# Column 0 multiplied centred and scaled afterwards, with the identity made on GpSimd and the first rows loaded in two halves

## The chip, the cores and the metric

The kernel runs on one core of a Trainium2 chip. The metric is the device time of one execution in microseconds (us). The profiled span, from the first to the last instruction of the profile, is about 1.7 us shorter than that time. Ratios, medians and ranges: runs that count as slow (over 1.5% above the fastest of their kernel) are left out. Absolute times are compared within one chip only: the kernel before takes 179.2 to 180.3 us, depending on the chip.

A ratio is the mean time of one kernel's fast runs over the mean of the kernel before's fast runs of the same rounds, so it is not quite the ratio of the medians quoted beside it.

A load is *issued* when its queue takes it up and *lands* when its last byte has arrived; rows are *usable* when the first instruction that waits for them, the statistics on DVE, starts. The PE clock is *open* at full pace and *closed* at half pace.

Engines: PE is TensorE (PEld its weight loads), DVE is VectorE, ACT is ScalarE, POOL is GpSimd, SP is SyncE, which only issues loads and stores here.

## The reference, cut to what matters

```python
x  = A_x                                   # 1 x 2048 x 512, bf16
xn = (x - mean) / sqrt(var + 1e-5)         # over the 512
B  = (gelu(xn @ w_gate) * (xn @ w_up)) @ w_down      # 512 -> 1792 -> 512
A  = irfft2(rfft2(xn) * (w_r + 1j * w_i))            # a filter over both axes
out = x + A + B
```

The kernel cuts the 2048 rows into 16 "columns" of 128 rows. The first two products, `g` (gate) and `u` (up), need `xn` of a column transposed, and weight chunks of 128 output features. The filter's row tables come partly from six GpSimd gathers.

## The kernel before

A small list scheduler inside the kernel orders the instructions of each engine by priorities and estimated durations. The start is what the change touches. Loads (cut):

```python
    load_x(0, 1)                                    # 128 rows x 512, 128 KB, SyncE
    d_ident = load_ct("ident", "ident", "ACT")      # identity for transposes, 32 KB
    load_x(1, 1)
    load_w(0, 2, ("SP", "ACT"))                     # Wg and Wu, chunks 0 and 1: 256 KB each
    ...
    load_x(2, 2)
    load_w(2, 4)
    ...
```

Layer norm of a column, then transposes on PE (cut):

```python
s  = bn_stats(x_t[:, c]);  ag = bn_aggr(s)          # DVE: mean and variance
e  = tensor_scalar(var + EPS)                       # DVE
r  = nc.gpsimd.tensor_tensor(ve, half, op=pow)      # POOL: 1/std
xn = tensor_scalar(x_t, mean, rstd, subtract, mult) # DVE, in two halves
...  # nc.tensor.transpose x4, copied to xnT by ACT and DVE; then glu(c)
```

While PE has nothing useful to do it multiplies a constant tile ("warm"), which is meant to have its clock open in time (here this starts at 1.34 us, and the clock opens at 7.11). The gathers wait for column 11 to be normalised:

```python
            d_tw.append(dma(P * n * 2, lambda ...: gather(k, s, c, a, n),
                            [g_idx] + XN[11], 20, eng="POOL", issue=1.2))
```

Of the kernel before, what the change touches and what calls it, by code (L numbers as in the profile page):

```python
# [10 lines left out]
P = 128  # L11
# [6 lines left out]
S = 2048  # L18
# [106 lines left out]
class _Op:  # L125
    __slots__ = ("eng", "dur", "fn", "deps", "prio", "new", "use", "lag", "n", "start", "end", "kind", "nbytes")


class _Plan:
# [7 lines left out]
    def op(self, eng, dur, fn, deps=(), prio=0.0, new=(), use=(), lag=0.0, nbytes=0):  # L137
        o = _Op()
        o.eng, o.dur, o.fn, o.prio, o.lag, o.nbytes = eng, dur, fn, prio, lag, nbytes
        o.deps = [d for d in deps if d is not None]  # L140
        o.new = list(new)
        o.use = list(new) + [b for b in use if b not in new]
        for b in o.use:
            b.users += 1
        o.n, o.start, o.end = len(self.ops), None, None
        self.ops.append(o)
        return o

    def run(self):
# [11 lines left out]
        while left:  # L161
            nxt, moved = None, False
            for e, ops in waiting.items():
                if not ops:
                    continue
                if t_eng[e] > now + 1e-9:
                    nxt = t_eng[e] if nxt is None else min(nxt, t_eng[e])
                    continue
                best = None
                for o in ops:  # L170
                    if any(d.end is None for d in o.deps):
                        continue
                    at = max([d.end + d.lag + self.HOP for d in o.deps if d.eng != "PE" or o.eng != "PE"] + [0.0])
                    if o.nbytes and o.eng != "POOL" and len(lanes) >= 8:
                        at = max(at, sorted(lanes)[-8])
                    if at > now + 1e-9:
                        nxt = at if nxt is None else min(nxt, at)
                        continue
                    held = [rings[b.tag][-self.bufs[b.tag]] for b in o.new if len(rings[b.tag]) >= self.bufs[b.tag]]
                    if any(b.free is None for b in held):  # L180
                        continue
                    at = max([b.free for b in held] + [0.0])
                    if at > now + 1e-9:
                        nxt = at if nxt is None else min(nxt, at)
                        continue
                    if best is None or (o.prio, o.n) < (best.prio, best.n):
                        best = o
                if best is None:
                    continue
                o, moved = best, True  # L190
                o.start = now
                o.end = now + o.dur
                t_eng[e] = o.end
                if o.nbytes:
                    wire = max(wire, o.end + 1.0) + o.nbytes / 0.34e6
                    o.end = wire + 1.0
                    if o.eng != "POOL":
                        lanes.append(o.end)
                    lanes = [x for x in lanes if x > now]
                for b in o.new:  # L200
                    rings[b.tag].append(b)
                for b in o.use:
                    b.left -= 1
                    if not b.left:
                        b.free = o.end + o.lag + self.HOP
                ops.remove(o)
                order.append(o)
                left -= 1
# [10 lines left out]
def kernel(  # L219
# [36 lines left out]
    Bs = pc.tile([P, 4, 2 * NG, NC, 2, 4], BF16, name="Bs", tag="Bs")  # L256
    RF_t = pc.tile([P, NC, P], BF16, name="RF_t", tag="RF")
# [7 lines left out]
    eps = pc.tile([P, 2], F32, name="eps")  # L265
    tiles = {}

# [45 lines left out]
    def load_x(c0, n, eng="SP", deps=()):  # L313
        q = nc.sync if eng == "SP" else nc.scalar
        o = load(n * P * D * 2, lambda: q.dma_start(out=x_t[:, c0:c0 + n], in_=x_v[:, c0:c0 + n]), deps, eng=eng)
        for c in range(c0, c0 + n):
            XD[c] = o

    def load_w(f0, f1, engs=("SP", "SP")):
        a, b = f0 * P, f1 * P  # L320
        os = []
        for t, v, e in ((Wg_sb, wg_v, engs[0]), (Wu_sb, wu_v, engs[1])):
            q = nc.sync if e == "SP" else nc.scalar
            os.append(load(NE * P * P * 2 * (f1 - f0),
                           lambda t=t, v=v, q=q: q.dma_start(out=t[:, :, a:b], in_=v[:, :, a:b]), eng=e))
        for f in range(f0, f1):
            WD[f] = os
# [6 lines left out]
    load_x(0, 1)  # L334
    d_ident = load_ct("ident", "ident", "ACT")
    load_x(1, 1)
    load_w(0, 2, ("SP", "ACT"))
    add("ACT", 1.3, lambda: nc.scalar.activation(out=eps[:, 1:2], in_=eps[:, 0:1], func=AF.Gelu_apprx_tanh),
        (o_eps,), -900)
    load_x(2, 2)  # L340
    load_w(2, 4)
    load_w(4, 6)
    load_x(4, 4)
    load_w(6, 10)
    load_x(8, 4)
    load_w(10, 14)
# [15 lines left out]
    def gather(k, s, c, a, n):  # L362
# [5 lines left out]
    Wd_sb = pc.tile([P, NFC, D], BF16, name="Wd_sb")  # L368
# [3 lines left out]
    o_mem = [add("POOL", 0.3, lambda: nc.gpsimd.memset(warm[:], 1.0), (), -20, lag=0.05),  # L372
             add("POOL", 0.2, lambda: nc.gpsimd.memset(half[:], -0.5), (), -15, lag=0.05)]  # L373
    wb = _Buf("S")
    NWARM, NGAP, GAP = 10, 1, 4
# [15 lines left out]
    XN, XT = {}, {}  # L391
# [6 lines left out]
    def layernorm(c0, n, due, after=(), halves=1):  # L398
        k = slice(c0, c0 + n)
        ag = []  # L400
        for c in range(c0, c0 + n):
            s = dve(0.6, lambda c=c: stats(c), [XD[c]] + list(after), due - 3.0 + 0.01 * (c - c0))
            ag.append(dve(0.15, lambda c=c: V.bn_aggr(out=mv[:, c], in_=tiles["st", c][:]), (s,), due - 3.2, ))
        e = dve(0.07, lambda: V.tensor_scalar(  # L404
            out=ve[:, k], in0=mv[:, k, 1], scalar1=EPS, scalar2=None, op0=ALU.add), ag, due - 5)
        r = add("POOL", 0.55, lambda: nc.gpsimd.tensor_tensor(  # L406
            out=rstd[:, k], in0=ve[:, k], in1=half[:, k], op=ALU.pow), (e, o_mem[1]), due - 5, lag=0.1)
        for c in range(c0, c0 + n):
            XN[c] = []
            for h in range(halves):  # L410
                d = slice(h * D // halves, (h + 1) * D // halves)
                XN[c].append(dve(0.04 + 0.29 / halves, lambda c=c, d=d: V.tensor_scalar(  # L412
                    out=xn[:, c, d], in0=x_t[:, c, d], scalar1=mv[:, c, 0:1], scalar2=rstd[:, c:c + 1],
                    op0=ALU.subtract, op1=ALU.mult), (r,), due - 2.5))
        return ag

    def pe_transpose(c, due):
        XT[c] = []
        b = _Buf("S")
        n = len(XN[c])  # L420
        for h in range(n):
            es = range(h * NE // n, (h + 1) * NE // n)

            def mm(h=h, es=es):
                if h == 0:
                    psum(f"tp.{c}", [P, NE, P], BF16)
                for e in es:
                    nc.tensor.transpose(tiles[f"tp.{c}"][:, e], xn[:, c, e * P:(e + 1) * P], ident)

            def ev(es=es, eng=(nc.scalar.copy, V.tensor_copy)[h]):  # L430
                eng(out=xnT[c // 4][:, es[0]:es[-1] + 1, c % 4], in_=tiles[f"tp.{c}"][:, es[0]:es[-1] + 1])

            o = pe(0.24 / n, mm, (XN[c][h], d_ident), due - 2, new=(b,) if h == 0 else (), use=(b,))
# [6 lines left out]
    first = layernorm(0, 1, -28, (), 2)  # L440
    layernorm(1, 1, -25, first)
    for c in range(4):
        if c == 2:
            layernorm(2, 2, -22, XT[0])
        pe_transpose(c, -28 + 3 * c)
        if c < NGAP:
            dummies(GAP, -29.9 + 3 * c, XN[c], P)
    for c0, n, due in ((4, 2, 14), (6, 2, 16), (8, 4, 24), (12, 4, 32)):
        layernorm(c0, n, due)
        for c in range(c0, c0 + n):  # L450
            dma_transpose(c, due)
        if c0 == 6:
            d_rf = load(P * NC * P * 2, lambda: nc.sync.dma_start(
                out=RF_t[:], in_=rf_d.rearrange("p (c k) -> p c k", c=NC)), XN[7])
            load_x(12, 4, deps=XN[7])
# [5 lines left out]
    for k in range(2):  # L461
        for c, s, a, n in ((2, 1, 0, 7 * KC), (0, 0, 0, KC), (1, 1, 7 * KC, KC)):
            d_tw.append(dma(P * n * 2, lambda k=k, c=c, s=s, a=a, n=n: gather(k, s, c, a, n),
                            [g_idx] + XN[11], 20, eng="POOL", issue=1.2))
# [20 lines left out]

    def glu(c0, n, f0, nf=1, extra=()):
# [10 lines left out]
        def mm(nm, W, tag, a, b):  # L497
            if a == 0:
                psum(f"{nm}.{key}", [P, D], tag=tag)
            for f in range(a, b):  # L500
                for e in range(NE):
                    nc.tensor.matmul(tiles[f"{nm}.{key}"][:, f * w:f * w + w], lhsT=W[:, e, (f0 + f) * P:(f0 + f + 1) * P],  # L502
                                     rhs=rhs(e), start=(f + e == 0), stop=(f == nf - 1 and e == NE - 1),
                                     skip_group_check=nf > 1)

        g = [o for c in range(c0, c0 + n) for o in XT[c]]
        step = min(nf, 2)
        us = []
        for a in range(0, nf, step):
            deps = g[-1:] if a else g  # L510
            new = [([], []), ([gb], [ub])][a == 0]
            g = [pe(step * dur, lambda a=a: mm("g_ps", Wg_sb, "G", a, a + step), deps + [WD[f0 + a][0]], t,
                    new=new[0], use=(gb,))]
            us = [pe(step * dur, lambda a=a: mm("u_ps", Wu_sb, "U", a, a + step), us + g + [WD[f0 + a][1]], t,
# [22 lines left out]
    FIRST = [(0, 1, 0, 4), (1, 1, 0, 4), (0, 2, 4, 2), (2, 2, 0, 2), (2, 2, 2, 2), (2, 2, 4, 2)]  # L537
    for c, n, f, nf in FIRST + [(0, 4, f, 1) for f in range(6, NFC)]:
# [8 lines left out]
    def fold(cg, t):  # L547
# [27 lines left out]
        for q in range(4):  # L575
            sb = _Buf("S")

            def mm(q=q):
                bp, xf = psum(f"bp.{cg}.{q}", [P, 4, P]), tiles[f"xf.{cg}"]
                for j in range(4):  # L580
                    nc.tensor.matmul(bp[:, j], lhsT=xf[:, j, q, :], rhs=RF_t[:, 4 * cg + j, :], start=True, stop=True)  # L581

            def ev(q=q):
                o = Bs[:, q].rearrange("p g c r a -> p (c r) g a")[:, 8 * cg:8 * cg + 8]
# [32 lines left out]
    def dstep(G, t):  # L617
        sb, db = _Buf("S"), _Buf("ds")

        def mm():  # L620
            dp = psum(f"dp.{G}", [P, 2, 2, P])
            work(f"ds.{G}", [P, D], "ds")
            for q in range(4):
                nc.tensor.matmul(dp[:, q % 2, q // 2], lhsT=Bs[:, q, G].rearrange("p c r a -> p (c r a)"),  # L624
# [173 lines left out]
    def load_ri():  # L798
# [4 lines left out]
    d_wd = [dma(P * 7 * D * 2, lambda k=k: nc.sync.dma_start(  # L803
        out=Wd_sb[:, 7 * k:7 * k + 7], in_=wd_v[:, 7 * k:7 * k + 7]), [PS_[3, q] for q in range(4)], 71 + k)
        for k in range(2)]
# [48 lines left out]
    def down(c, t):  # L854
# [8 lines left out]
        for k in range(len(cuts) - 1):  # L863
# [5 lines left out]
            def mm(k=k, s=s, tag=tag):  # L869
                y = psum(f"yp_.{c}.{k}", [P, D], tag=tag)  # L870
                for f in range(NFC):
                    nc.tensor.matmul(y[:, s], lhsT=tiles[sb, f][:, cl * P:(cl + 1) * P], rhs=Wd_sb[:, f, s],  # L872
# [54 lines left out]
```

## Time and profile before

| | before |
|---|---|
| time, median of 3 runs | 180.27 us (180.09 to 180.38) |
| profiled span (of a further run, which took 179.39 us) | 177.6 us |
| PE busy | 173.4 us, 98% |
| first byte of a load | 1.72 us |
| first useful matmul | 6.89 us |

The page's first part, busy time and share of the span:

```profile
span 177.6 us, 3041 instructions
PE 173.4 (98%) x1100; PEld 92.9 (52%) x1100; DVE 118.1 (66%) x266; ACT 87.4 (49%) x158; POOL 18.6 (10%) x33
```

The chain of waits of the kernel before, its first 12 us; columns are start, duration and what ran:

```profile
1.34 4.44 PE warm L380 x10
5.79 0.64 PE tp L428 x4
...
6.89 0.82 PE g_ps L502 x8
7.72 0.45 PE u_ps L502 x8
8.16 0.22 PE tp L428 x4
8.39 0.45 PE g_ps L502 x8
8.83 0.01 issue
8.84 0.62 PE u_ps L502 x8
9.46 0.45 PE g_ps L502 x8
...
10.80 0.45 PE u_ps L502 x8
11.25 0.45 PE tp L428 x8
```

From 1.34 us on the whole chain is PE. The first eight g matmuls take 0.82 us and every later eight 0.45: the clock opens in between, at 7.11 us. From there on nothing is lost but 0.18 us at 8.84, for Wu chunks 2 and 3, and 0.28 us near 76. So only the time ahead of the useful work can be won. By 11.25 us both columns 0 and 1 have their first g and u.

The timeline of DVE before, where the rows arrive (start, duration, instruction, and in brackets how long the engine stood idle and for what):

```profile
3.51 0.69 DVE L396 BATCH_NORM_STATS2 st<-x_t 128x6 f32<-128x512 bf16 x1 [3.51 <-DMA x_t<-in_A_x_dram]
5.38 0.60 DVE L412 TENSOR_SCALAR xn<-x_t,mv,rstd 128x256 bf16<-128x256 bf16 x2
```

### The profile page before, as it was taken

What the parts mean: (1) busy time and instruction counts of PE and PEld (TensorE: products, weight loads), DVE (VectorE), ACT (ScalarE), POOL (GpSimd) and SP (SyncE); (2) the same over time, 40 slices, a digit from 0 to 9 for tenths busy, and PEclk for the clock granted to TensorE, in tenths of its full rate; (3) what the DMA queues carried; (4) which work ended last, traced back from release to release, by engine and by line L of the source; (5) the groups of instructions that cost most, each with busy time, mean ns of one, the idle gap of its engine ahead of it and who ended that gap; (6) DMA issues with size and microseconds to landing.
All of it is one profiled execution on the core that took longest, in us unless ns stands there. A gap on an engine that the chain in (4) does not pass through costs nothing.

```text
span 177.6 us, 3041 instructions
## 1 busy us (share of the span) xinstructions
PE 173.4 (98%) x1100; PEld 92.9 (52%) x1100; DVE 118.1 (66%) x266; ACT 87.4 (49%) x158; POOL 18.6 (10%) x33
## 2 busy tenths in 40 slices
PE   6999999999999999999999999999999999999993
PEld 2598545545554544554555455554445444544463
DVE  1869999999537995889999885336442541632522
ACT  3162437456789737999998855453111211211100
POOL 3212138743200000000000000000000000000000
PEclk9999999999999999999999999999999999999999
DMA  5999487999297001302211121100222221322212
GB/s 144 311 355 359 86 270 84 223 296 193 52 347 255 2 0 29 93 2 59 61 48 37 37 59 37 27 0 0 84 68 66 83 89 59 92 80 69 74 45 59
DMA packets 23182, 19.24 MB, mean 108 GB/s; under 512 B 8512, under 2 KB 21824, under 8 KB 23168
## 3 DMA queue, kind: packets, MB, share of 16 engines
q1 hardware_dynamic: 22176, 17.57, 35.0%
q0 software_dynamic: 320, 1.19, 3.1%
q10 hardware_dynamic: 672, 0.30, 0.6%
q8 instruction: 8, 0.13, 0.3%
q14 instruction: 6, 0.05, 0.1%
HBM read 13.28 MB, written 2.10 MB: 87 GB/s over the span
## 4 chain that ended last, share of the span: by engine, by line
PE 91%; ACT 3%; DVE 3%; issue 1%; POOL 0%; DVEq 0%; POOLq 0%
PE u_ps L502 25%; PE g_ps L502 25%; PE warm L380 3%; ACT E L652 2%; PE yp L818 2%; PE bp L581 2%; PE gp L767 2%; PE yp__2078 L872 2%; PE yp__1994 L872 2%; PE yp__1967 L872 2%; PE yp__1936 L872 2%; PE yp__1909 L872 2%; PE yp__1820 L872 2%; PE yp__1793 L872 2%; PE yp__1762 L872 2%; PE yp__1735 L872 2%
## 5 line engine op out<-in xcount | busy, mean ns | idle before, releaser
L502 PE MATMUL g_ps<-xnT,Wg_sb 128*128 128x512 bf16 (+2 forms) x264 | 58.1, 347 | 0.0
L502 PE MATMUL u_ps<-xnT,Wu_sb 128*128 128x512 bf16 (+2 forms) x264 | 57.9, 347 | 0.0
L527 DVE TENSOR_TENSOR hT<-u_ps,ge 128x512 bf16<-128x512 f32 x56 | 38.4, 685 | 17.5 <-PE u_ps L502 14.4
L519 ACT ACTIVATE ge<-g_ps 128x512 bf16<-128x512 f32 x56 | 33.5, 598 | 30.5 <-PE g_ps L502 26.5
L502 PEld LDWEIGHTS <-Wu_sb 128*128 128x128 bf16 x264 | 24.3, 98 | 22.3 <-DMA Wu_sb<-in_B_w_up_dram 0.2
L502 PEld LDWEIGHTS <-Wg_sb 128*128 128x128 bf16 x264 | 24.3, 98 | 20.7 <-issue 0.2
L872 PEld LDWEIGHTS <-hT 128*128 128x128 bf16 x252 | 23.0, 98 | 21.9
L824 ACT CAST yf<-yp 128x512 bf16<-128x512 f32 x16 | 9.3, 586 | 37.6 <-PE yp L818 37.6
L652 ACT CAST E<-ep 64x512 bf16<-64x512 f32 x32 | 18.5, 579 | 1.1 <-PE ep L646 0.7
L396 DVE BATCH_NORM_STATS2 st<-x_t 128x6 f32<-128x512 bf16 x16 | 10.5, 676 | 4.8 <-DMA x_t<-in_A_x_dram 4.8
L629 ACT CAST ds<-dp 128x512 bf16<-128x512 f32 x16 | 8.8, 589 | 1.1 <-PE dp L624 1.0
L773 ACT CAST Gs<-gp 128x512 bf16<-128x512 f32 x16 | 8.6, 593 | 1.0 <-PE gp L767 1.0
L406 POOL TENSOR_TENSOR rstd<-ve,half 128x2 f32<-128x2 f32 (+2 forms) x7 | 6.6, 949 | 21.9 <-DVE ve L404 21.9
L585 ACT CAST Bs<-bp 128x512 bf16<-128x512 f32 x16 | 8.3, 603 | 0.5 <-PE bp L581 0.5
L818 PEld LDWEIGHTS <-Gs 128*128 128x128 bf16 x64 | 4.8, 98 | 3.5
L380 PE MATMUL warm<-warm 128*128 128x512 bf16 (+1 forms) x14 | 5.1, 539 | 1.3 <-POOL half L373 1.3
L412 DVE TENSOR_SCALAR xn<-x_t,mv,rstd 128x512 bf16<-128x512 bf16 (+1 forms) x17 | 6.1, 399 | 0.3 <-POOL rstd L406 0.3
L818 PE MATMUL yp<-CT,Gs 128*128 128x128 bf16 x64 | 6.0, 219 | 0.0
L683 DVE TENSOR_TENSOR m<-X,TW 128x1024 bf16<-128x1024 bf16 x8 | 5.5, 692 | 0.2
L624 PEld LDWEIGHTS <-Bs 128*128 128x128 bf16 x64 | 4.4, 98 | 2.4
L689 DVE TENSOR_TENSOR m<-X,TW 128x1024 bf16<-128x1024 bf16 x8 | 5.5, 684 | 0.0
L646 PE MATMUL ep<-ds,CT 128*128 128x512 bf16 x16 | 5.4, 379 | 0.0
(103 smaller groups left out, 169.0 us busy)
## 6 DMA issues: line engine op xcount, KB each, us to landing
y<-in_A_x_dram SPq DMA_DIRECT2D x16, 128.0 KB, 2.1
F<-F SPq DMA_DIRECT2D x32, 64.0 KB, 2.0
out_dram<-y SPq DMA_DIRECT2D x15, 128.0 KB, 1.7
Wd_sb<-in_B_w_down_dram SPq DMA_DIRECT2D x2, 896.0 KB, 8.3
x_t<-in_A_x_dram SPq DMA_DIRECT2D x3, 512.0 KB, 6.8
Wg_sb<-in_B_w_gate_dram SPq DMA_DIRECT2D x2, 512.0 KB, 6.8
Wu_sb<-in_B_w_up_dram SPq DMA_DIRECT2D x2, 512.0 KB, 9.1
Wg_sb<-in_B_w_gate_dram SPq DMA_DIRECT2D x3, 256.0 KB, 5.1
```

What stands on the lines that cost most here:

```text
L380: nc.tensor.matmul(tiles["warm"][:, 0:w], lhsT=warm[:, 0:P], rhs=warm[:, 0:w], start=True, stop=True)
L396: V.bn_stats(out=st[:], in_=x_t[:, c])
L502: nc.tensor.matmul(tiles[f"{nm}.{key}"][:, f * w:f * w + w], lhsT=W[:, e, (f0 + f) * P:(f0 + f + 1) * P], rhs=rhs(e), start=(f + e == 0), ...
L519: nc.scalar.activation(out=e[:, 0:nf * w], in_=tiles[f"g_ps.{key}"][:, 0:nf * w], func=AF.Gelu_apprx_tanh)
L527: V.tensor_tensor(out=out, in0=tiles[f"u_ps.{key}"][:, 0:nf * w].rearrange("p (f w) -> p f w", w=w) if nf > 1 else tiles[f"u_ps.{key}"][:, ...
L585: nc.scalar.copy(out=o, in_=tiles[f"bp.{cg}.{q}"][:].rearrange("p c (r g a) -> p (c r) g a", r=2, a=4))
L629: nc.scalar.copy(out=ds[:].rearrange("p (s k t) -> p s k t", s=2, t=2), in_=tiles[f"dp.{G}"][:].rearrange("p s t k -> p s k t"))
L652: nc.scalar.copy(out=tiles[f"E.{g}"][64 * h:64 * h + 64, r], in_=tiles[f"ep.{g}.{h}"][64 * r:64 * r + 64])
L773: nc.scalar.copy(out=o, in_=tiles[f"gp.{g}.{h}"][:].rearrange("p q (n a) -> p (q n) a", a=4))
L818: nc.tensor.matmul(yp[:, q], lhsT=tiles["G"][:, q, c], rhs=IQ[q], start=(q == 0), stop=(q == 3), skip_group_check=True)
L824: nc.scalar.copy(out=tiles[f"yf.{c // 2}"][:, c % 2], in_=tiles[f"yp.{c}"][:])
L872: nc.tensor.matmul(y[:, s], lhsT=tiles[sb, f][:, cl * P:(cl + 1) * P], rhs=Wd_sb[:, f, s], start=(f == 0), stop=False)
```

## The change

The intent: (x − m)·s times W equals s·((x − m) times W), so column 0 can go to PE as soon as its mean is known, and be scaled by s = 1/std afterwards. This takes the variance and the power on GpSimd off the way to the first matmul. Around it the loads, the first matmuls' order and some dependences are rearranged. The core of the diff:

```diff
-    load_x(0, 1)
-    d_ident = load_ct("ident", "ident", "ACT")
-    load_x(1, 1)
-    load_w(0, 2, ("SP", "ACT"))
+    d_ident = add("POOL", 0.3, lambda: nc.gpsimd.affine_select(out=ident, in_=warm[:, 0:P], ...))
+    load_x(0, 1, 2.95, p1=P // 2)                  # rows 0-63 on SP
+    load_x(0, 1, 2.95, "ACT", p0=P // 2)           # rows 64-127 on ACT
+    load_x(1, 1, 3.5, "ACT")
+    d_g = [load_first(e, eng) for e, eng in ((0, "SP"), (1, "ACT"), (2, "SP"), (3, "ACT"))]
+    load_x(2, 2, 6.4)
+    d_u = load(..., Wu_sb[:, :, 0:4 * P] ..., land=7.4)       # Wu chunks 0 to 3 in one load, 512 KB
 ...
+    def column0():                                 # stats, aggregate, then x - mean in two halves
+    def xm_transpose(c, os): ...                   # 4 transposes of the centred column
+    def spread(c): ...                             # one fp32 matmul spreads 1/std over partitions
+    glu_first(0, 0, 4):                            # g, u of column 0: 4 chunks; DVE scales both, then gelu
 ...
-            d_tw.append(... gather ..., [g_idx] + XN[11], ...)
+            d_tw.append(... gather ..., [g_idx] + XN[3], ...)
```

The numbers 2.95, 3.5, 6.4, 7.4 tell the kernel's own scheduler when each load lands. Column 0 is also normalised and transposed in the old way, later, for its other chunks and for the filter. Warm-up matmuls fall from ten to seven. Column 3's moments move to ACT.

## The prediction

> **What bounds the kernel now.** TensorE. The page's first part gives PE 173.4 us busy of a 177.6 us span. The chain of waits is PE for 91%. In that chain the first useful matmul (g_ps) starts at 6.89 us and the last ends near 174.9 us. From the spacings in the timeline (216 ns for 512 columns, 108 for 256, 56 for 128) the matmuls in between add up to about 167.1 us. So after 6.89 us under 1 us is lost: about 0.4 us because the first eight g matmuls ran at half pace (0.82 us instead of 0.45), 0.2 us for a Wu load, a few tenths near 71 to 76 us. Another 2.7 us is the tail after the last matmul. What can be won is the time before 6.89 us.
>
> **What the change does there.** Before, in the timeline: x lands at 3.51; stats 0.69, aggregate 0.18, variance 0.15, GpSimd power 0.58 (4.76 to 5.34), normalise two halves 0.60, transposes from 5.78, copy on ACT 0.37, g at 6.89.
> After: column 0 needs only its mean before the transposes.
> - First rows in two halves on two queues, nothing ahead of them: the 32 KB identity load landed 2.2 us after issue, the 128 KB one took 2.7; I estimate x at 3.05 (-0.45).
> - Variance and power leave the chain (about -0.9). But in VectorE's new order the statistics of column 1 (0.69 + 0.18 + 0.15) stand ahead of the two copies of the transposes (0.29 each). I estimate the copies at 5.7 to 6.3 and g from 6.05: 0.8 us earlier, not 1.3.
> - The identity by GpSimd must be ready by 4.5 us. It starts near 1.3, so it should be.
>
> **What it costs PE.** Four more transposes (0.22)[...]; warm-up matmuls fall from ten to seven, off the useful path. The columns streamed for g and u are unchanged, with 64 more 128-column matmuls at slightly more overhead each (about 0.1 us net).
>
> **The clock.** The timeline shows matmul spacing going from half to full pace near 7.1 us. [...] So of the useful work brought ahead of 7.1 us, half is lost: about 0.4 us of the 0.8. [...]
>
> **Later.** VectorE in 6 to 12 us gets two fp32 scalings and a multiply (0.69 each). I expect a short wait of PE (0.1 to 0.3 us) for normalised column 2 near 10 us. Column 3's moments on ACT and the earlier gathers should fit in slack; weights are needed later than they land. Sum by 11.5 us: PE about 0.3 us ahead of before. The rest of the kernel streams as before, give or take 0.4 us of scheduling luck.
>
> **Prediction.** 180.0 us, range 178.9 to 181.2; faster by over 2%: 0.03, within 2%: 0.94, slower: 0.03.
>
> **What would show it.** Timeline: x statistics near 3.05; first g near 6.05; second-half g at 56 ns spacing only after about 7.1; u of column 1 done near 11.2 (before: 11.25), with one transpose group of four left instead of eight. Chain of waits: PE still over 88%.
>
> **What would make it wrong.** [...] the reordered filter stage (60 to 80 us) stalling PE on VectorE or ACT, or no longer stalling it.

The sum came to a lead of about 0.3 us by 11.5 us, and the forecast to 180.0 us. One term of PE's cost is cut, the fp32 matmul that spreads 1/std, because the trace before the change has none to read a time from; measured afterwards at an open clock, it takes 0.28 us (a_x1_wu_clock). That the clock would open near 7.1 us again, as in the trace before, was the estimate.

## The result, and the profile after

On the chip of the first result the kernel after took 182.90 us (182.60 to 183.28, five runs), the kernel before 180.09 us (180.00 to 180.38, five runs); the ratio is 1.0160, 95% interval 1.0137 to 1.0182. It is correct. That is slower by 1.6%, outside the predicted range of 178.9 to 181.2.

The page's first part of the kernel after:

```profile
span 181.3 us, 3147 instructions
PE 173.9 (96%) x1136; PEld 96.5 (53%) x1153; DVE 121.1 (67%) x272; ACT 88.8 (49%) x163; POOL 18.0 (10%) x36
```

PE has only 0.5 us more to do; the span is 3.7 us longer. (The two profiled runs took 183.05 and 179.39 us; the medians are only 2.8 us apart.) The difference is standing still, so the chain of waits must tell where. The chain after, its first 20 us:

```profile
0.80 2.94 DMA x_t<-in_A_x_dram
3.74 0.02 issue
3.75 6.55 DMA Wu_sb<-in_B_w_up_dram
10.30 0.05 issue
10.35 1.07 PE u_ps L584 x16
...
12.53 0.89 PE u_ps L636 x16
...
17.18 0.62 PE g_ps L636 x10
17.80 0.36 issue
18.16 0.39 PE g_ps L636 x4
18.55 0.34 issue
18.89 0.27 PE g_ps L636 x2
```

Before, the chain held no load in these 12 us. Now it runs over the first rows, then over the first Wu load, which lands at 10.3 us; u of column 1 ends at 13.43 instead of 11.25. At 17.80 and 18.55 PE stands although the profile shows nothing that it waits for ("issue"). The timelines of DVE and PE after:

```profile
4.02 0.69 DVE L413 BATCH_NORM_STATS2 st<-x_t 128x6 f32<-128x512 bf16 x1 [4.02 <-DMA x_t<-in_A_x_dram]
5.31 0.61 PE L500 MATMUL tm<-CT,scr_w 128*128 128x128 bf16 x4 [0.51 <-DVE scr_w L484]
6.76 1.86 PE L584 MATMUL g_ps<-scr_w,Wg_sb 128*128 128x128 bf16 x16 [0.42 <-DVE scr_w L503]
8.95 1.06 PE L459 MATMUL tp<-CT,xn 128*128 128x128 bf16 x8
10.35 1.07 PE L584 MATMUL u_ps<-scr_w,Wu_sb 128*128 128x128 bf16 x16 [0.34 <-DMA Wu_sb<-in_B_w_up_dram]
```

The rows are usable at 4.02 us, not at 3.05 as predicted, and 0.51 us later than before. g starts at 6.76. Its sixteen matmuls take 1.86 us; the same sixteen of u, at full pace, take 1.07. The first byte of any load moves at 2.13 us (1.72 before, of the identity); the first byte of the rows at 2.13 on ACT's queue and 2.40 on SP's (1.83 before).

The sum for this pair of traces: both columns have their first g and u 2.18 us later (13.43 against 11.25), less four of column 2's transposes that are done by then (0.22); the two pauses lose 0.52 and 0.50 us against the regular spacing; two filter products near 33 and 50 us wait 0.55 and 0.20 us for DVE; before's 0.28 us near 76 is gone. That is 3.45 of the 3.7 us. (Regular steps of 0.22 us every 9 us in this trace are matmul records that are missing, not time.)

### The profile page after: what moved, and what is told of

It reads as the page before. It is cut to its first block, busy times and chain, and to the rows that moved or that the text cites. A ratio compares the mean times of both kernels' runs of the same rounds, so it can differ in the third digit from the quotient of the medians.

```text
span 181.3 us, 3147 instructions
## 1 busy us (share of the span) xinstructions
PE 173.9 (96%) x1136; PEld 96.5 (53%) x1153; DVE 121.1 (67%) x272; ACT 88.8 (49%) x163; POOL 18.0 (10%) x36
## 4 chain that ended last, share of the span: by engine, by line
PE 91%; DMA 5%; DVE 1%; issue 1%
PE g_ps L636 26%; PE u_ps L636 26%; DMA Wu_sb<-in_B_w_up_dram 4%; PE bp L716 2%; PE gp L904 2%; PE dp L761 2%; PE yp L957 2%; PE ep L783 2%; PE yp__2123 L1011 2%; PE yp__2065 L1011 2%; PE yp__1980 L1011 2%; PE yp__1949 L1011 2%; PE yp__1891 L1011 2%; PE yp__1806 L1011 2%; PE yp__1747 L1011 2%; PE yp__2149 L1011 2%
## 5 line engine op out<-in xcount | busy, mean ns | idle before, releaser
L636 PE MATMUL g_ps<-xnT,Wg_sb 128*128 128x512 bf16 (+2 forms) x265 | 56.1, 337 | 1.1 <-issue 0.7
L636 PE MATMUL u_ps<-xnT,Wu_sb 128*128 128x512 bf16 (+2 forms) x267 | 56.0, 337 | 0.3
L661 DVE TENSOR_TENSOR hT<-u_ps,ge 128x512 bf16<-128x512 f32 x55 | 37.6, 685 | 16.9 <-PE u_ps L636 15.5
L653 ACT ACTIVATE ge<-g_ps 128x512 bf16<-128x512 f32 x55 | 32.8, 599 | 30.3 <-PE g_ps L636 25.3
L439 POOL TENSOR_TENSOR rstd<-ve,half 128x1 f32<-128x1 f32 (+2 forms) x7 | 6.0, 855 | 23.1 <-DVE ve L421 20.0
L445 DVE TENSOR_SCALAR xn<-x_t,mv,rstd 128x512 bf16<-128x512 bf16 (+1 forms) x15 | 5.4, 401 | 0.3 <-POOL rstd L439 0.3
L397 PE MATMUL warm<-warm 128*128 128x512 bf16 (+1 forms) x13 | 4.0, 484 | 1.4 <-POOL warm L344 1.4
L904 PEld LDWEIGHTS <-F 128*128 128x128 bf16 x64 | 4.2, 98 | 1.9
```

Source lines behind the costliest of these rows:

```text
L636: nc.tensor.matmul(tiles[f"{nm}.{key}"][:, f * w:f * w + w], lhsT=W[:, e, (f0 + f) * P:(f0 + f + 1) * P], rhs=rhs(e), start=(f + e == 0), ...
L653: nc.scalar.activation(out=e[:, 0:nf * w], in_=tiles[f"g_ps.{key}"][:, 0:nf * w], func=AF.Gelu_apprx_tanh)
L661: V.tensor_tensor(out=out, in0=tiles[f"u_ps.{key}"][:, 0:nf * w].rearrange("p (f w) -> p f w", w=w) if nf > 1 else tiles[f"u_ps.{key}"][:, ...
```

## The experiments

Eighteen kernels ran, in five batches, each on its own chip. All gave correct results. The theories at the start were: (T1) the first rows in two halves come late; (T2) the first Wu load is needed before it lands; (T3) the clock opens late, because PE idles early; (T4) narrow matmuls bring the pauses of PE near 18 us.

### Batch 1, chip 9: the kernel after, and three single remedies

**a_same** is the kernel after, unchanged.

> The changed kernel unchanged, with a new trace, to see which of the losses repeat. Theory: 182.6 to 183.3 us again; u of column 0 again starts after 9.5 us because its 512 KB load lands near 10 us; the clock opens near 10 us[...]; two pauses of TensorE of about 0.5 us each near 18 us, in the 128-column matmuls of column 3, again. Rival (one bad execution: stray slow DMA packets): load lands near 7.5 us, no pauses, time nearer 181.

Measured: 180.28 us over five runs (a sixth, 183.67, counts as slow; before on this chip 179.23), ratio 1.0068, interval 1.0049 to 1.0087. So the first chip's 1.6% is not the same everywhere. In this trace the rows are usable at 3.48, g starts at 6.23 at full pace, and there are no pauses near 18 us. PE's timeline shows what is left:

```profile
6.23 1.05 PE L584 MATMUL g_ps<-scr_w,Wg_sb 128*128 128x128 bf16 x16 [0.42 <-DVE scr_w L503]
7.12 0.44 PE L513 MATMUL r<-scr_r 128*128 128x128 f32 x2
7.40 0.61 PE L459 MATMUL tp<-CT,xn 128*128 128x128 bf16 x8
9.02 1.07 PE L584 MATMUL u_ps<-scr_w,Wu_sb 128*128 128x128 bf16 x16 [1.01 <-DMA Wu_sb<-in_B_w_up_dram]
```

g is 0.66 us ahead of the kernel before, as intended, and then PE stands 1.01 us for Wu. The lead is more than lost.

**a_clock** adds warm-ups: `dummies(NWARM, -100, last=2)` and `dummies(4, -29.9, o_xm, P, last=5)`, where the last of a group emits that many matmuls.

> The changed kernel with one more 512-column warm-up and four more 128-column ones placed where TensorE was idle before column 0's first g. Nothing else moves. Theory[...]: clock opens near 6.5 to 7.1 us; alone this gains under 0.3 us as long as u of column 0 waits for its load until about 10.3 us. Rival (the clock's late opening is what costs the 2 us): 1 us or more gained.

Measured: 180.34 us, four runs from 179.99 to 182.38 (two more, 183.31 and 183.67, count as slow), ratio 1.0100 (1.0056 to 1.0143). No gain. In its trace the clock was open anyway and g waited 0.6 us for Wg, u 0.4 us for Wu.

**a_wu** issues the first Wu load ahead of rows 2 and 3:

```diff
-    load_x(2, 2, 6.4)
     d_u = load(... Wu_sb[:, :, 0:4 * P] ..., land=7.4)
+    load_x(2, 2, 6.4)
```

> The changed kernel with the 512 KB load of Wu's first four chunks issued before the load of rows 2 and 3 instead of after. Theory (u of column 0 waits for that load): it lands 1 to 3 us earlier, u of column 0 starts at 9.7 instead of 10.35 us with the clock still shut, gain 0.4 to 0.7 us. Rival (the load is late because of slow packets, not its place): no gain.

Measured: 181.08 us, ratio 1.0111 (1.0096 to 1.0125): no gain, a miss for T2 alone. The Wu wait is gone, but the rows came late (statistics at 4.21), PE idled before 6.96, and the clock, open since 4.25, closed again from 7.66 to 11.07: u's sixteen matmuls took 1.86 us, where full pace takes 1.07.

**a_first** puts a wide block of matmuls ahead of column 3's narrow one:

```diff
-    FIRST = [..., (2, 1, 0, 4), (3, 1, 0, 4), (0, 2, 6, 2), ...]
+    FIRST = [..., (2, 1, 0, 4), (0, 2, 6, 2), (3, 1, 0, 4), ...]
```

> The changed kernel with the wide block (columns 0 and 1, chunks 6 and 7) put ahead of the narrow block of column 3. Theory[...]: the pauses shrink from 1.0 us to under 0.3, total gains 0.7 to 1.0 us. Rival (they wait for data or for a buffer of column 3): the pauses stay with column 3.

Measured: 181.19 us, ratio 1.0108 (1.0094 to 1.0123). It has no pauses, but neither has a_same on this chip: inconclusive for T4.

### Batch 2, chip 11: halves and identity in the kernel before

**a_land** tells the scheduler the landings that were measured (Wu 9.2 instead of 7.4 us, later loads 1 to 1.5 us later), so that it puts g of column 1 ahead of u of column 0.

> The changed kernel with its own scheduler told landings as measured (Wu's first four chunks at 9.2 us instead of 7.4, the later ones about 1 us later than before). It then puts g of column 1 before u of column 0, so TensorE has 0.9 us of other work while Wu is on its way. Theory (in fast runs the loss of the change is u of column 0 waiting 1.0 to 1.7 us for Wu): the wait in front of that u shrinks to under 0.6 us and the time falls by 0.4 to 0.9 us against the changed kernel, to about 179.6 to 180.1 where the kernel before takes 179.2. Rival (the loss is the added work on TensorE and VectorE): no gain.

Measured: 181.47 us (before 179.43), ratio 1.0099 (1.0073 to 1.0125). A miss: u of column 0 no longer waits for Wu, but PE now waits for the normalised columns 1 and 2 (0.34, 0.35 and 0.48 us lost). That is the trace of the fastest run, 179.87, which by itself met the forecast; the other five took 181.21 to 181.67, and what they lost no trace shows.

**a_x1** loads the first rows whole:

```diff
-    load_x(0, 1, 2.95, p1=P // 2)
-    load_x(0, 1, 2.95, "ACT", p0=P // 2)
+    load_x(0, 1, 2.95)
```

> The changed kernel with the first rows loaded by one transfer on one queue instead of two halves on two queues; the order of everything else is the same. Theory (the halves bring nothing: first byte at 2.13 us in four traces against 1.72 before): first byte near 1.8 us, statistics of column 0 start at 3.3 to 3.5 us as with halves, time the same within 0.3 us. What the prediction assumed (halves land 0.45 us earlier): statistics at 3.9 us or later, 0.4 us slower.

Measured: 180.37 us, ratio 1.0049 (1.0026 to 1.0071). The first byte moves at 1.81 us instead of 2.13, and the issue takes 0.40 us instead of 0.58. But the rows were usable only at 3.88: single packets took 450 to 690 ns, where most take 46. The ratio is no better than that of the unchanged kernel on chips without pauses (1.0050 and 1.0068).

**b_gps** is the kernel before with the identity made by GpSimd (the diff's `affine_select`), **b_gps_half** the same with the first rows in two halves:

```diff
-    load_x(0, 1)
+    XD[0] = load(P * D * 2, lambda: [q.dma_start(out=x_t[p:p + 64, 0:1], in_=x_v[p:p + 64, 0:1])
+                                     for q, p in ((nc.sync, 0), (nc.scalar, 64))])
```

> The kernel before with the identity made on GpSimd instead of loaded; the order of instructions on all engines is otherwise unchanged. Theory (off the critical path, but it takes a 32 KB load of 256-byte packets out of the way): time the same within 0.3 us, perhaps 0.1 faster; the identity is ready by 2 us. Rival[...]: power of column 0 starts later than 4.76 us, slower.

> As b_gps, and the first rows in two halves on two queues. The pair isolates the halves without the rest of the change. Theory: first byte 0.2 to 0.4 us later than in b_gps, statistics no earlier, time the same or up to 0.3 us slower. What the prediction assumed: statistics about 0.4 us earlier, time 0.2 to 0.4 us less.

Measured: b_gps 179.58 us, ratio 1.0013 (0.9999 to 1.0027): the identity costs nothing. b_gps_half 181.34 us, ratio 1.0100 (1.0078 to 1.0122). So the halves alone cost 1.76 us in the kernel before. The timelines of SP, DVE and PE, b_gps first:

```profile
0.80 0.87 SPq L315 DMA_DIRECT2D x_t<-in_A_x_dram  x2
3.42 0.69 DVE L399 BATCH_NORM_STATS2 st<-x_t 128x6 f32<-128x512 bf16 x1 [3.42 <-DMA x_t<-in_A_x_dram]
5.84 0.54 PE L431 MATMUL tp<-CT,xn 128*128 128x128 bf16 x4 [0.22 <-DVE xn L415]
```

and b_gps_half:

```profile
0.80 0.58 SPq L334 DMA_DIRECT2D x_t<-in_A_x_dram  x1
4.27 0.69 DVE L400 BATCH_NORM_STATS2 st<-x_t 128x6 f32<-128x512 bf16 x1 [4.27 <-DMA x_t<-in_A_x_dram]
6.73 0.54 PE L432 MATMUL tp<-CT,xn 128*128 128x128 bf16 x4 [1.70 <-DVE xn L416]
```

Half the bytes took longer to issue (0.58 us against 0.87 for two whole loads, 0.40 and 0.42), but so did the whole load of the next rows behind the half (0.81), and the rows were usable 0.85 us later. After the 1.70 us in which PE stood, its clock closed, which cost a second time. The view of windows gives busy times of the engines in each stretch, then the granted clock (PEclk); first b_gps, then b_gps_half:

```profile
7.40:10.90 3.50, 3.50 (x64) 3.37 (x62) 2.94 (x9) 1.25 (x3) 0.70 (x1) 1.00 1.12 342
```

```profile
7.40:10.90 3.50, 3.26 (x32) 3.05 (x30) 2.19 (x7) 0.87 (x2) 0.92 (x2) 0.51 1.15 320
```

In the same 3.5 us PE did 64 matmuls at clock 1.00 and 32 at 0.51. The trace's clock record has it closed from 7.47 to 10.88, that is 3.41 us. From 4.00 to 7.40 us, ahead of that, PE was busy for only 1.70 us (2.89 in b_gps). One caution: ahead of the first clock record this view shows 1.00 also where matmuls run at half pace (in the kernel after, for the 1.86 us of g's sixteen matmuls from 6.76), so there the pace itself has to be read.

### Batch 3, chip 15: both load remedies together

**a_again** is the kernel after. **a_x1_wu** loads the first rows whole, and Wu in two parts ahead of rows 2 and 3:

```diff
-    load_x(2, 2, 6.4)
-    d_u = load(... Wu_sb[:, :, 0:4 * P] ..., land=7.4)
+    d_u = [load(... Wu_sb[:, e:e + 2, 0:4 * P] ..., land=7.4) for e in (0, 2)]
+    load_x(2, 2, 7.0)      # and u's first half waits for the first part only
```

**a_x1_wu_clock** adds a_clock's warm-ups to that. **b_gps_half_sp** is b_gps_half with both halves issued by SP.

> The kernel after, unchanged, again, so that the repaired kernels of this batch have it beside them on one chip. Earlier chips gave ratios to the kernel before of 1.016 and 1.007. Expected: 1.005 to 1.016, first byte of a load near 2.1 us, statistics of column 0 at 3.4 to 4.1 us, a wait of 0.5 to 3 us for the first Wu load ahead of u of column 0, and some runs at a granted clock of 0.99 or below. Theory (late data: halves and Wu): it is slower than the repaired kernel of this batch by 0.8 us or more. Rival (the late scaling itself costs it): within 0.3 us of the repaired one.

> The kernel after with both suspected parts undone: the first rows loaded whole on one queue, and the first Wu load in two parts by input chunks, ahead of the load of rows 2 and 3, so that u of column 0 can begin on the first part. Theory (late data are the cause): first byte near 1.8 us, statistics near 3.5 us, g near 6.2 us, u of column 0 by 8.3 us with no Wu wait over 0.2 us, and 178.9 to 179.6 us, that is a ratio to the kernel before of 0.998 to 1.002. Rival (the late scaling costs by itself: more PE work and a fuller VectorE early): 1.004 to 1.006, as the kernel with only the first rows whole (1.0049).

> The kernel a_x1_wu with more warm-up matmuls: one more of 512 columns at the start and four more of 128 columns behind the centering. Theory[...]: clock opens near 5.5 to 6.5 us and stays open, every run at a granted clock of 0.995 or more, spread of the runs under 0.6 us, and 0.2 to 0.6 us faster than a_x1_wu. Rival (the clock is decided by when rows and weights land, the warm-ups do not matter): no difference over 0.3 us, as with the unrepaired kernel, where they gained nothing.

> The kernel before, with the identity by GpSimd and the first rows in two halves of 64 partitions, both issued by SyncE one after the other. With the halves on two queues it was 1.0100 of the kernel before, with rows whole 1.0013. Theory A (a load of 64 partitions is slow by itself: its issue takes 0.58 us instead of 0.43): both issues take 0.55 us or more, first byte near 2.1 us, second half 0.5 us behind it, statistics 4.0 us or later, ratio 1.006 to 1.014. Theory B (two queues issuing at the same time slow each other): issues of 0.40 to 0.45 us, first byte near 1.8 us, statistics 3.5 to 3.9 us, ratio 1.001 to 1.005.

| kernel | median us (range) | ratio (95%) |
|---|---|---|
| before (ten runs; 181.86 counts as slow) | 180.09 (179.14 to 181.59) | |
| a_again | 182.16 (181.87 to 183.78) | 1.0138 (1.0089 to 1.0186) |
| a_x1_wu | 181.67 (181.47 to 183.48) | 1.0103 (1.0052 to 1.0153) |
| a_x1_wu_clock | 181.60 (181.52 to 181.72) | 1.0083 (1.0045 to 1.0121) |
| b_gps_half_sp | 183.28 (182.59 to 184.50) | 1.0190 (1.0143 to 1.0238) |

Neither theory was met by a_x1_wu. The Wu wait is gone, but its rows were usable only at 4.32, and its clock was closed from 7.70 to 11.11. The warm-ups did what they should here: in spite of rows at 4.29 the clock opened at 6.59 and stayed open, and there were no runs at 183.48 like the two of a_x1_wu (mean of six 182.21 without, 181.62 with). Only one of these two shows a lower granted clock (0.991), and the medians do not differ. b_gps_half_sp fits neither forecast wholly: its two issues take 1.21 us together, as Theory A says of a half, but the first byte, at 1.89 us, is one of Wu's on ACT's queue: the rows' own first packet starts at 2.79 (1.81 in b_gps). The halves land at 4.25 and 4.53, so being issued second is not the reason, and the rows are usable at 4.63. The halves lose on one queue too; why is not shown.

The surprise was that the pauses of PE were back: 0.49 and 0.46 us lost in a_again, 1.14 in a_x1_wu, 0.46 and 0.48 in a_x1_wu_clock, between 16 and 19.4 us. So this is a matter of the chip, and a repair of the loads cannot mend it. In a_again ACT had stood for 3.10 us as well, put down to "remote" by the profile, which names no engine or load. The first six kernels of the after type on chips 9 and 11 had none of this. What lies there in all of them is the six gathers on GpSimd, which the change starts at 11 to 14 us instead of 27 (a changed dependence, one word in the diff).

### Batch 4, chip 6, and batch 5, chip 0: the gathers

**a_gather** (a_gather3 is the same kernel) takes that one word back. The order of instructions on PE, DVE, ACT and SP stays what it was:

```diff
-                            [g_idx] + XN[3], 20, eng="POOL", issue=1.2))
+                            [g_idx] + XN[11], 20, eng="POOL", issue=1.2))
```

**b_gather** makes the opposite edit in the kernel before. **a_x1_wu_gather** is a_x1_wu with the gathers held back. **a_again2** and **a_again3** are the kernel after, as controls.

> The kernel after, unchanged, as a control beside a_gather. If this chip is one of those with pauses: TensorE stands 0.3 us or more twice between 16 and 19 us, ratio to the kernel before 1.013 to 1.017. If it is one without them: ratio 1.005 to 1.009.

> The kernel after with its six GpSimd row gathers held back to where the kernel before has them (behind column 11 normalised); TensorE, ScalarE, VectorE and SyncE keep their order. Theory[...]: no pause between 16 and 19 us, no stand of ScalarE there, no wait near 32 us, and where a_again2 shows pauses this one is 1 to 2 us faster. Rival 1[...]: the pauses stay, and no gain over 0.3 us. Rival 2 (pauses are the chip's): they come and go in both.

> The kernel after with first rows whole, first Wu load in two parts and ahead of rows 2 and 3, and the gathers held back. Theory (the loss is made of these three): ratio to the kernel before 0.997 to 1.002. Rival (scaling column 0 late costs by itself, 0.5 to 0.8 us): 1.003 to 1.006.

> The kernel before with nothing but its gathers brought forward, behind column 3 normalised as in the kernel after. Theory[...]: pauses of 0.3 us or more of TensorE or ScalarE between 14 and 24 us on a chip where a_again2 has them, ratio 1.003 to 1.010. Rival (only narrow matmuls together with gathers do it, and this kernel has none there): 0.998 to 1.002, no pauses.

(What is left to test is that early gathers bring the pauses, or, as rival 1, that narrow matmuls alone do.)

| kernel, chip 6 | median us (range) | ratio (95%) |
|---|---|---|
| before | 179.53 (179.04 to 180.02) | |
| a_again2 | 180.37 (179.87 to 181.11) | 1.0050 (1.0027 to 1.0073) |
| a_gather | 180.63 (180.07 to 181.48) | 1.0062 (1.0036 to 1.0088) |
| a_x1_wu_gather | 179.72 (179.61 to 181.41) | 1.0027 (0.9997 to 1.0056) |
| b_gather | 180.46 (179.98 to 181.26) | 1.0052 (1.0028 to 1.0076) |

This chip has no pauses in the kernel after, so a_gather could not lose any, and did not gain. Two things were still learned. With all three suspects removed the kernel is as fast as the kernel before in four of six runs (179.61 to 179.72); the other two took 181.23 and 181.41 (the latter is the profiled one: rows at 4.13, clock open only at 10.41). And b_gather shows a second price of early gathers, without any pause. PE's waits in it, from 12 to 40 us (what waited, for what, us in total, times, longest):

```profile
PE u_ps L502 <- DVE hT L527: 0.7, 1, 0.7
PE bp L581 <- DMA RF_t<-spec_rf: 0.2, 1, 0.2
```

and the DVE instruction that made it wait:

```profile
18.81 0.69 DVE L396 BATCH_NORM_STATS2 st<-x_t 128x6 f32<-128x512 bf16 x1 [1.53 <-DMA x_t<-in_A_x_dram]
```

Two things meet here. The scheduler, which places the powers of later columns between the gathers, has moved this statistic ahead of the product that PE waits for. And its rows landed late: the load was issued at 8.03 us and landed at 18.79, where in the kernel before it was issued at 8.09 and landed at 17.25. The gathers' own transfers (1.18 MB) move from 14.4 to 22.8 us here, while it is on its way. On this chip the pair a_again2 and a_gather, with one order on PE, DVE, ACT and SP, shows the same: the last Wu load lands at 23.33 with early gathers and at 19.95 with late ones.

The last batch repeated the pair on another chip.

> The kernel after, unchanged, control for a_gather3. With pauses of TensorE of 0.3 us or more twice between 16 and 19 us: ratio 1.013 to 1.017; without: 1.004 to 1.009.

> The kernel after with its gathers held back, as a_gather. Theory (gathers cause the pauses): no pauses, and 1 us or more faster than a_again3 where that one has them. Rival (the pauses have nothing to do with the gathers): within 0.4 us of a_again3, with pauses where that one has them.

Chip 0 does have the pauses. Before took 179.95 us (179.59 to 181.64 over ten runs; 182.74 counts as slow), a_again3 182.51 (182.27 to 183.57), ratio 1.0139 (1.0096 to 1.0182); a_gather3 181.82 (180.79 to 182.49), ratio 1.0067 (1.0022 to 1.0112). Timelines of PE and ACT in a_again3:

```profile
16.00 1.16 PE L636 MATMUL g_ps<-xnT,Wg_sb 128*128 128x128 bf16 x14
17.57 0.22 PE L636 MATMUL g_ps<-xnT,Wg_sb 128*128 128x128 bf16 x1 [0.41 <-issue]
18.30 0.22 PE L636 MATMUL g_ps<-xnT,Wg_sb 128*128 128x128 bf16 x1 [0.52 <-issue]
18.28 1.08 ACT L653 ACTIVATE ge<-g_ps 128x512 bf16<-128x512 f32 x2 [3.89 <-remote]
```

The same block in a_gather3:

```profile
16.62 1.06 PE L636 MATMUL g_ps<-xnT,Wg_sb 128*128 128x128 bf16 x16
17.51 1.06 PE L636 MATMUL u_ps<-xnT,Wu_sb 128*128 128x128 bf16 x16
17.71 0.60 ACT L653 ACTIVATE ge<-g_ps 128x512 bf16<-128x512 f32 x1 [1.19 <-PE g_ps L636]
```

The pauses and the stand of ACT are gone with the gathers, and 0.7 us of the median and 1.05 us of the mean (182.70 to 181.65) with them. That is one trace of each, and the rows were late in a_gather3 (usable at 4.17, against 3.46); the two ranges of times and the two intervals of the ratio just overlap. Over all traces: of the twelve of the after type with early gathers five have pauses, on chips 15 and 0 and on that of the first result, and none on chips 9, 11 and 6; of the seven traces with late gathers (of either type) none has. So the pauses were seen only with early gathers on a chip that is prone to them. b_gather, the kernel before with early gathers, has none, but ran only on a chip where a_again2 has none either. Whether the gathers on GpSimd themselves stop PE and ACT, and how, is not shown: PE's instruction loads are in the trace, one starts at 13.9 to 16.7 us in every trace, it takes as long with pauses (1.11 to 1.18 us) as without (1.07 to 1.18), and it has landed before the pause. This stays open, and T4 with it: it was neither shown nor refuted that narrow matmuls are needed as well.

## Why the prediction was wrong, point by point

- **What bounds the kernel** was right: PE, and only the time ahead of its useful stream can be won. PE's added work was right too (0.5 us busy).
- **"First rows in two halves on two queues ... I estimate x at 3.05 (-0.45)" failed first.** The estimate was read off between the landings of a 32 KB and a 128 KB load, as if a half were simply a smaller load. Measured: 3.46 to 4.39 us in the eleven traces with the kernel after's split rows. The half on ACT's queue did land as estimated (3.09 to 3.17 us in the seven traces that show it); the half on SP's queue, issued at the same moment, landed at 3.36 to 3.45 in six traces, which is no gain on the whole load before (3.48), and at 3.92 to 4.29 in the other five. And in the kernel before the halves made the rows 0.85 us later and the kernel 1.76 us slower. Each half took 0.55 to 0.58 us to issue where a first whole load took 0.40, and SP issued its next load at 1.43 us in the kernel after, at 1.25 in a_x1. But halves are not all of it: in the four traces of the after type with whole rows these are usable at 3.88 to 4.32. What else in its load order delays them (the second rows and Wg pieces on ACT's queue are the candidates) was not separated.
- **"Weights are needed later than they land" failed second.** It hardly held even in the kernel before, where u starts with 256 KB of Wu at 7.55 and the second 256 KB was already 0.18 us short at 8.84. Glu of column 0 now asks for all 512 KB at about 8.0 us where the rows are early, and with the kernel after's order of loads they land at 9.0 to 10.3. The simplest case is a_again2, with early rows, an open clock and no pauses: g is 0.6 us ahead of the kernel before (6.28 against 6.89), then PE stands 1.39 us for Wu. The balance, 0.8 us, is what that chip shows (180.37 against 179.53).
- **The clock** was named as a risk (in a passage that is cut), and rightly. In the first result's trace it opens at 9.96 us instead of 7.11, so that g takes 1.86 us where full pace takes 1.07. What goes with it is late rows. In all nine traces whose statistics start by 3.54 us the clock opens at 4.5 to 7.1 us and stays open. Of the eleven that start at 3.88 or later, five have it closed again for 3.41 us (PE was busy for 1.63 to 2.12 of the 3.40 us from 4.00 in these, for 2.54 to 3.37 in the nine with early rows; but in a_again, at full pace from 7.13 on, for 1.76), and four open it only at 9.7 to 10.5 (of the other two, a_x1_wu_clock has more warm-ups and a_again no clock record). The granted clock of every run is on record too, and one such closed stretch goes with 0.990 or 0.991 in the five traces. From its length and the half pace I estimate that it costs up to 1.7 us. A clock of 0.989 to 0.991 stands in 20 of 74 runs with split rows (three of them count as slow), but in 1 of 91 with whole rows, 55 of them of the kernel before; on chip 11 alone in 3 of 6 runs of b_gps_half and in none of b_gps. More warm-ups are no cure: a_clock has it in 3 of 6 runs. How much of the scatter of the times comes from late rows is still argued and not shown, since only the profiled run of each kernel shows its rows.
- **"The earlier gathers should fit in slack" failed third.** GpSimd has the slack (busy for 18.0 us, 10% of the span, in the kernel after); the DMA has less: the last Wu load lands at 20.9 to 24.3 us in the seven traces with early gathers that show it, at 19.3 to 20.2 in the six with late ones. And on the chip of the first result, and on chips 15 and 0, pauses come with them. For a_again3 the sum is 0.8 us of the Wu balance as above, 1.25 us of pauses, 0.70 us of later waits for DVE, less before's 0.28 near 76: 2.5 us, against 2.56 measured.
- **The variance and power off the chain, and the harmless identity** were right: where rows were early, g starts at 6.20 to 6.30 in all six traces, 0.6 us ahead (0.8 had been predicted), and b_gps is within 0.13% of the kernel before. The `affine_select` that makes the identity took 0.28 to 0.29 us and started at 1.43 to 1.45 us.

What the late scaling itself costs or gains is bounded, not settled: with rows whole, Wu split and early, and gathers late, most runs are 0.1 to 0.2 us behind the kernel before. No kernel here beats it. The obvious next one, a_x1_wu_gather with the warm-ups of a_x1_wu_clock, was not run.

## What to carry to other kernels

When a change moves the first use of data forward, list every load that is then needed, with its bytes and its measured landing, and look for the next one that becomes the limit: here 0.6 us of lead ran into a weight load that was 1.4 us late. Load rows whole: here the halves made the kernel before 1.76 us slower. A late first load can cost a second time, through the PE clock: in five of the eleven traces here with late rows it closed again for 3.41 us, in none of the nine with early ones. And test a change of a bystander, such as moved gathers, on more than one chip and by itself: here one changed word moved the ratio from 1.0067 to 1.0139 on one chip and by nothing that could be measured on another. Behind a few transfers moved forward, other loads can land later, though the engine that issues them has time to spare: here the last Wu load landed at 23.33 us with early gathers and at 19.95 with late ones (a_again2 and a_gather).
